# Stage weights of a list-scheduled kernel changed, and one expert matrix's high halves moved from GpSimd to ScalarE

## The chip, the cores and the metric

The kernel runs on one core of a Trainium2 chip. The time is the device time of one execution, in microseconds. The engines are named as in the profile: PE (TensorE, its matmuls), PEld (its weight loads), DVE (VectorE), ACT (ScalarE), POOL (GpSimd) and SP (SyncE, which here only issues transfers). Each runs its own instructions strictly in the order in which they stand in its queue.

## The reference

All inputs are float32. Three stages follow each other.

```python
# 1: delta-rule attention, B=2, H=8, S=768, D=48
k_n = k / (norm(k) + 1e-6)
for t in range(S):
    y[:, :, t] = q_t @ state
    state += beta_t * outer(k_t, v_t - state.T @ k_t)
# 2: gated MLP with mixing over the sequence, d_model 384, d_ff 1024
u, v = split(gelu_tanh(x @ w_in))
x = x + (u * (w_sg @ (layernorm(v) * g_ln) + b_sg)) @ w_out
# 3: one of 8 experts per token, 384 -> 1024 -> 384
e = argmax(x @ w_gate), or the expert of the token before it
    where sigmoid(x @ w_local) >= 0.5
out = p[e] * (relu(x @ w1[e]) @ w2[e])
```

## The kernel before

**One program, ordered by a planner.** The code does not issue instructions as it is written. Each operation is recorded in a `Plan` with its engine, an estimated cost and what it depends on, and at the end `emit()` places all of them, engine by engine. Whenever an engine is free it takes, of the operations that could start within 120 ns of the earliest, the one with the highest sum of its rank (the length of the chain of work that hangs on it) and its bias. The bias is a number per stage, from the table `BIAS`, set by `at(name)` or by the steps of the attention. Every recorded operation carries the line L371 in the profile, so the line tells nothing there, and tiles and shapes have to. All of the working memory is one tile, `arena`, with fixed addresses (`AT`); the matmul banks are `x_80` to `x_85`, a ring of six that all stages share, and two banks `s`.

**Attention.** Time is cut into six tiles of 128 steps. K0 to K5 load and normalise k and make its products, X0 to X2 invert a triangular system on DVE by forward substitution (X0 in blocks of 16, which `join` puts together in T0 and T1), T0 to T5 make the tiles' update matrices on PE, C0 to C5 run the recurrence, and B0 to B2 load beta. W0 to W5 load the six parts of `w_in` and turn them into f16, each with six instructions of 128x512 on DVE through a single raw buffer `w64_512`.

**Halves.** A float32 matmul is made of three f16 matmuls. `split()` makes the two halves: the high half is the value rounded to f16, by the engine that the caller names ("a" is ACT, "p" is POOL, else DVE), and the low half is the rest, for all scaled weights by one `scalar_tensor_tensor` on DVE, which reads the raw tile and the high half.

**MLP and experts.** The stages in0, u0, sp0, out0 do the MLP of the first batch row, in1 to out1 that of the second; prep readies `w_sg` and `w_out`. route0 and route1 build the lists of tokens for each expert; early and late run experts 0 and 1. Then the experts 2 to 6, one more block for an expert with too many tokens (the "list expert", chosen from the data), and expert 7 follow (experts). `load_expert` fetches w1 as three raw tiles of 128x1024 (512 KB) and w2 as four of 128x768 (384 KB), through a ring of three raw buffers, and splits them in pieces of 512 columns: six 128x512 pieces for w1, four 128x512 and four 128x256 for w2. Its operations are the stages load0 (experts 0 and 1) and load (the other seven). Four sets of split weights exist, so an expert's weights can be made while others are used. In `run_blocks`, each of four banks of w1's products takes a relu on ACT, which makes the high half of the hidden values, and a low half on DVE; w2's product is scaled by ACT into `ob`, and POOL writes it to `out` by an indirect DMA (a scatter, `DMA_INDIRECT out_dram<-arena`).

POOL makes the high halves of both matrices, and its queue also holds the gathers and the scatters. The loop over further lists behind the program's main part (`For_i`) runs zero times with this data.

Of the kernel before, what the change touches and what calls it, by code (L numbers as in the profile page):

```python
# [16 lines left out]
def make_split(nc):  # L17
    def split(hi, lo, src, s, he, le):
# [12 lines left out]


ORDER = "K0 K1 B0 X0 K2 K3 B1 X1 T0 T1 C0 C1 K4 K5 B2 X2 T2 T3 C2 C3 T4 T5 C4 C5 W0 W1 W2 W3 W4 W5"
BIAS = {"K0": 5e5, "K1": 5e5, "X0": 4.5e5, "K": 4.5e5, "X": 2e5, "T": 3e5, "C": 4e5, "Q": 3e5, "N": 6e5, "W": 1e5, "B0": 4.7e5, "B": 3e5, "prep": 5e4,
        "in0": 1.4e5, "u0": 1e5, "sp0": 1e5, "out0": 1e5, "in1": 1.2e5, "u1": 8e4, "sp1": 8e4, "out1": 8e4, "load0": -2e5, "route0": 1.5e5, "early": -1e5, "route1": 3e5, "late": -1e5, "list": -2e5,
        "load": -2e5, "gather": 0.0, "experts": 0.0, "rest": -3e5}
SLOTS = 4
WORDS = 46400

# [565 lines left out]
def attention(plan, A, P, q, k, v, beta, x_all, idf, filler):  # L605
# [28 lines left out]

    was, plan.bias = plan.bias, BIAS["N"]
    one = A.tile([128, 1], F32, "one")
# [91 lines left out]
    def stage2(gi):  # L728
# [28 lines left out]
        for j in range(0 if sets[0] in FINE else 31):  # L757
            for eng, lo, hi_, tg, sz in ((nc.vector, 0, min(j + 1, C0), "tmp", TMP), (nc.gpsimd, C0, j + 1, "tmpp", TMPP)):
# [104 lines left out]
    def stage4(b, t):  # L863
# [9 lines left out]
        for c in range(2):  # L873
# [20 lines left out]
            if ci < 2 * NT - 1:  # L894
# [56 lines left out]
def model_kernel(ctx, tc, q, k, v, beta, w_in, g_ln, w_sg, b_sg, w_out, w_gate, w_local, w1, w2, out):  # L951
    nc = tc.nc
    B, H, S, D = q.shape
# [19 lines left out]
    early = ExitStack()  # L973
# [13 lines left out]
    def split(*a):  # L987
        make_split(nc)(*a)
# [306 lines left out]
    def load_expert(fetch, slot, step=512):  # L1295

        W = [ep.tile(SHAPES[nm], F16, tag=f"{nm}{slot}", name=nm, bufs=1) for nm in SHAPES]
        w1h, w1l, w2h, w2l = W
        flat = lambda x: x.rearrange("p a b -> p (a b)")
        for kc in range(KD):  # L1300
            raw = ep.tile([128, F2], F32, tag="raw1", name="raw1", bufs=3)
            fetch(raw, w1, slice(kc * 128, (kc + 1) * 128))
            for c0 in range(0, F2, step):
                cs = slice(c0, c0 + step)
                split(w1h[:, kc, cs], w1l[:, kc, cs], raw[:, cs], 64.0, "p", "v")
        for qd in range(4):
            n = NF2 // 4
            raw = ep.tile([128, F2], F32, tag="raw1", name="raw2", bufs=3)[:, :n * DM].rearrange("p (n d) -> p n d", n=n)
            fetch(raw, w2, slice(qd * n * 128, (qd + 1) * n * 128))
            for c0 in range(0, n * DM, step):  # L1310
                cs = slice(c0, min(c0 + step, n * DM))
                f = lambda x: flat(x[:, qd * n:(qd + 1) * n, :])[:, cs]
                split(f(w2h), f(w2l), flat(raw)[:, cs], 64.0, "p", "v")
        return W
# [4 lines left out]
    def fixed(e):  # L1319
        return lambda raw, w, rs: nc.sync.dma_start(raw, rows_of(w[e], rs))  # L1320
# [57 lines left out]
    def at(name):  # L1378
        plan.bias = BIAS.get(name, 0.0)

# [8 lines left out]
    for b in range(B):  # L1389
# [138 lines left out]
    with tc.For_i(NX, nv, 1) as i:  # L1528
# [5 lines left out]
        X, col = listed(lc, "loop")  # L1534
# [32 lines left out]
```

## Time and profile before

| | |
|---|---|
| time, median of 3 runs | 506.03 us (503.86 to 507.68) |
| the profiled execution | 506.47 us, span 504.8 us |
| busy: PE, DVE, POOL, ACT | 426.8, 363.6, 212.3, 184.1 us |
| mean granted TensorE clock | 0.928 |

The span is the part of an execution that the profiler's instructions cover; 1.7 us lie around it. Attention takes the first 194 us, the MLP runs to about 340 us, routing and the first two experts' blocks overlap it and end at 418 us, and the other experts end at 499 us. A row of a timeline gives the start, the length, the engine, the operation with its operands, and in brackets how long the engine had been idle and what ended that.

### The profile page before, as it was taken

What the parts mean: (1) busy time and instruction counts of PE and PEld (TensorE: products, weight loads), DVE (VectorE), ACT (ScalarE), POOL (GpSimd) and SP (SyncE); (2) the same over time, 40 slices, a digit from 0 to 9 for tenths busy, and PEclk for the clock granted to TensorE, in tenths of its full rate; (3) what the DMA queues carried; (4) which work ended last, traced back from release to release, by engine and by line L of the source; (5) the groups of instructions that cost most, each with busy time, mean ns of one, the idle gap of its engine ahead of it and who ended that gap; (6) DMA issues with size and microseconds to landing.
All of it is one profiled execution on the core that took longest, in us unless ns stands there. A gap on an engine that the chain in (4) does not pass through costs nothing.

```text
span 504.8 us, 16775 instructions
## 1 busy us (share of the span) xinstructions
PE 426.8 (85%) x7100; PEld 325.6 (64%) x7100; DVE 363.6 (72%) x824; ACT 184.1 (36%) x451; POOL 212.3 (42%) x373
## 2 busy tenths in 40 slices
PE   0467689969779899988989799999599999999593
PEld 0466688858769685555645566687488868777372
DVE  1796956689645687989689693678789987647770
ACT  2656335795743644332022241223132213312110
POOL 8413550073000003625476622443557455666551
PEclk9986756899976999989999999999999999999988
DMA  6743201104321543111652400170555466656530
GB/s 95 141 85 67 47 5 21 35 20 126 65 92 44 150 169 116 32 64 32 196 182 105 144 1 32 48 226 32 152 158 165 143 209 173 187 184 204 154 96 26
DMA packets 62191, 53.29 MB, mean 106 GB/s; under 512 B 43549, under 2 KB 55109, under 8 KB 62114
## 3 DMA queue, kind: packets, MB, share of 16 engines
q1 hardware_dynamic: 57730, 46.08, 32.4%
q0 software_dynamic: 2176, 5.71, 3.6%
q8 instruction: 57, 0.93, 0.7%
q10 hardware_dynamic: 2208, 0.40, 0.6%
q14 instruction: 20, 0.16, 0.1%
HBM read 46.27 MB, written 6.89 MB: 105 GB/s over the span
## 4 chain that ended last, share of the span: by engine, by line
PE 55%; DVE 17%; DMA 9%; issue 7%; ACT 4%; POOL 4%; SPq 2%; ACTq 0%; POOLq 0%; DVEq 0%
PE x L371 54%; DVE arena L371 17%; DMA arena<-in_moe_w_dram 4%; ACT arena L371 3%; POOL arena L371 3%; SPq L371 2%; DMA out_dram<-arena 2%; PE s L371 1%; DMA arena<-in_v_dram 1%; DMA arena<-in_moe_w_in_dram 1%; DMA arena<-in_k_dram 1%; DMA arena<-in_moe_w_sg_dram 1%; ACTq L371 0%; DMA arena<-in_beta_dram 0%; DVE x_all L371 0%
## 5 line engine op out<-in xcount | busy, mean ns | idle before, releaser
L371 PE MATMUL x<-arena 64*32 64x32 f32 (+8 forms) x6385 | 372.6, 243 | 45.0 <-DVE arena L371 21.1
L371 PEld LDWEIGHTS <-arena 128*128 128x128 f16 x2005 | 175.7, 99 | 101.0 <-issue 13.6
L371 DVE SCALAR_TENSOR_TENSOR arena<-arena 128x512 f16<-128x512 f32 (+6 forms) x186 | 123.9, 698 | 32.9 <-POOL arena L371 27.2
L371 POOL TENSOR_SCALAR arena<-arena 128x512 f16<-128x512 f32 (+2 forms) x146 | 91.3, 645 | 99.7 <-DVE arena L371 59.5
L371 PEld LDWEIGHTS x<-arena 64*32 64x32 f32 (+3 forms) x4416 | 99.0, 134 | 41.3 <-issue 15.7
L371 ACT ACTIVATE arena<-x 128x384 f16<-128x384 f32 (+5 forms) x137 | 63.5, 483 | 118.0 <-PE x L371 103.5
L371 POOL TENSOR_TENSOR arena<-arena 128x384 f32<-128x384 f32 (+14 forms) x117 | 61.5, 526 | 76.2 <-DVE arena L371 40.1
L371 DVE TENSOR_TENSOR arena<-arena 128x384 f16<-128x384 f32 (+40 forms) x213 | 82.0, 389 | 13.9 <-ACT arena L371 7.4
L371 ACT COPY arena<-x 32x128 f32<-32x128 f32 (+7 forms) x160 | 52.9, 355 | 48.4 <-PE x L371 37.9
L371 DVE SCALAR_TENSOR_TENSOR arena<-x,arena 128x384 f16<-128x384 f32 (+5 forms) x105 | 55.1, 548 | 15.5 <-ACT arena L371 8.1
L371 PE MATMUL x<-idf,arena 128*128 128x128 f32 x183 | 33.8, 332 | 19.6 <-DVE arena L371 19.5
L371 ACT ACTIVATE arena<-arena 128x384 f16<-128x384 f32 (+5 forms) x38 | 19.8, 527 | 59.8 <-POOL arena L371 47.1
L371 PEld LDWEIGHTS x<-idf,arena 128*128 128x128 f32 x183 | 26.4, 172 | 21.5 <-POOL arena L371 17.4
L371 POOL MEMSET arena<- 32x256 f32 (+13 forms) x43 | 14.7, 357 | 58.4 <-DVE arena L371 45.0
L371 DVE TENSOR_SCALAR arena<-arena 128x1 f32<-128x1 f32 (+9 forms) x83 | 25.0, 319 | 15.1 <-DMA arena<-in_beta_dram 8.8
L371 ACT ACTIVATE arena<-x,arena 128x384 f32<-128x384 f32 x17 | 9.8, 580 | 53.2 <-PE x L371 28.1
L371 ACT COPY arena<-arena 64x256 f32<-64x256 f32 (+2 forms) x60 | 26.1, 445 | 5.7 <-DVE arena L371 4.6
L371 POOL DMA_INDIRECT out_dram<-arena x17 | 19.3, 1136 | 19.1 <-ACT arena L371 14.3
L371 DVE TENSOR_TENSOR arena<-arena,x 128x192 f32<-128x192 f32 (+2 forms) x34 | 11.0, 325 | 17.3 <-PE x L371 12.9
L371 POOL DMA_INDIRECT arena<-x2d,arena x15 | 16.9, 1126 | 13.7 <-PE x L371 9.4
L371 DVE STREAM_TRANSPOSE arena<-arena 128x1024 f32<-128x1024 f32 x9 | 17.5, 1978 | 0.2
L371 PE MATMUL s<-arena 64*48 64x48 f32 x352 | 14.1, 223 | 1.2 <-ACT arena L371 1.0
(58 smaller groups left out, 148.6 us busy)
## 6 DMA issues: line engine op xcount, KB each, us to landing
arena<-in_moe_w_dram SPq DMA_DIRECT2D x27, 512.0 KB
arena<-in_moe_w_dram SPq DMA_DIRECT2D x36, 384.0 KB
arena<-in_moe_w_in_dram SPq DMA_DIRECT2D x6, 512.0 KB
arena<-in_v_dram SPq DMA_DIRECT2D x24, 96.0 KB
arena<-in_q_dram SPq DMA_DIRECT2D x24, 96.0 KB
arena<-in_moe_w_sg_dram SPq DMA_DIRECT2D x6, 384.0 KB
x2d<-x_all SPq DMA_DIRECT2D x12, 192.0 KB
arena<-in_k_dram SPq DMA_DIRECT2D x20, 96.0 KB
```

Of the source, the lines that this page charges most:

```text
L371: call(*[real(a) for a in args], **{k: real(a) for k, a in kw.items()})
```

## The change

Some 35 numbers of `BIAS` change, most of them of the attention's steps, which had shared a few numbers before and now have one each. Among the larger moves: K5 rises above K0, K1 falls below K0, B0 falls below the K steps, X2 falls from 2e5 to 27400 (below W0 to W5), in0 and sp0 rise, load rises from -2e5 to -148500, late rises a little and experts falls to -24300. Besides, the high halves of w1 are made on ACT where POOL made them: 54 instructions of 128x512 in the program that runs (nine loads of six).

```diff
-BIAS = {"K0": 5e5, "K1": 5e5, "X0": 4.5e5, "K": 4.5e5, "X": 2e5, "T": 3e5, "C": 4e5, "Q": 3e5, "N": 6e5, "W": 1e5, "B0": 4.7e5, "B": 3e5, "prep": 5e4,
...
-        "load": -2e5, "gather": 0.0, "experts": 0.0, "rest": -3e5}
+BIAS = {"W5": 52900.0, "W4": 104400.0, "W3": 100000.0, "W2": 38000.0, "W1": 100000.0, "W0": 69800.0, "B2": 135000.0, "B1": 395700.0, "C5": 443000.0, "C4": 434500.0, "C3": 408000.0, "C2": 473100.0, "C1": 400000.0, "C0": 397000.0, "T5": 320300.0, "T4": 300000.0, "T3": 300000.0, "T2": 307300.0, "T1": 300000.0, "T0": 300000.0, "X2": 27400.0, "X1": 200000.0, "K5": 646300.0, "K4": 435000.0, "K3": 447700.0, "K2": 450000.0, "K0": 500000.0, "K1": 479300.0, "X0": 4.5e5, "K": 4.5e5, "X": 2e5, "T": 3e5, "C": 4e5, "Q": 300000.0, "N": 600000.0, "W": 1e5, "B0": 417500.0, "B": 3e5, "prep": 50000.0,
...
+        "load": -148500.0, "gather": 0.0, "experts": -24300.0, "rest": -300000.0}
...
-                split(w1h[:, kc, cs], w1l[:, kc, cs], raw[:, cs], 64.0, "p", "v")
+                split(w1h[:, kc, cs], w1l[:, kc, cs], raw[:, cs], 64.0, "a", "v")
```

**At the start**, SP issues before the change four loads of k (K1, K0), four of beta, then the other sixteen of k. After it, all twenty loads of k stand first, the four of K5 in front, and then twelve of beta. ACT, which issues the other halves of K0 and K1, takes K0's first. On DVE, K0's whole normalisation now comes before K1's, and the one operation of X0 that reads beta stands behind K1's reductions instead of ahead of K0's first.

**DVE after X0**, before the change. The first row is the end of X0; the rows from `x_82` to `x_85` with 128x4x64 are the causal masks of C1's products, the transpose of 128x1024 opens X1, and the last row is T0's first step of joining its blocks:

```order
L371 STREAM_TRANSPOSE arena<-arena 128x32x32 x2
L371 TENSOR_TENSOR arena<-arena 128x16 x2
L371 TENSOR_SCALAR arena<-arena 128x16 x2
L371 RECIPROCAL arena<-arena 128x16 x2
L371 TENSOR_TENSOR arena<-x_82,arena 128x4x64
L371 TENSOR_TENSOR arena<-x_83,arena 128x4x64
L371 TENSOR_TENSOR arena<-x_84,arena 128x4x64
L371 TENSOR_TENSOR arena<-x_80,arena 128x4x64
L371 TENSOR_TENSOR arena<-x_81,arena 128x4x64
L371 TENSOR_TENSOR arena<-x_85,arena 128x4x64
L371 STREAM_TRANSPOSE arena<-arena 128x1024
L371 TENSOR_SCALAR arena<-x_82,arena 128x8x16
```

The same place after the change:

```order
L371 STREAM_TRANSPOSE arena<-arena 128x32x32 x2
L371 TENSOR_SCALAR arena<-arena 128x16
L371 RECIPROCAL arena<-arena 128x16 x2
L371 TENSOR_TENSOR arena<-arena 128x16 x2
L371 TENSOR_SCALAR arena<-arena 128x16
L371 RECIPROCAL arena<-arena 128x16
L371 TENSOR_TENSOR arena<-arena 128x16 x2
L371 TENSOR_SCALAR arena<-arena 128x16
L371 RECIPROCAL arena<-arena 128x16
L371 TENSOR_SCALAR arena<-x_82,arena 128x8x16
L371 TENSOR_TENSOR arena<-x_81,arena 128x4x64
L371 TENSOR_TENSOR arena<-x_83,arena 128x4x64
```

T0's step now comes ahead of the masks and of X1. Its next step, the additions, stands behind three operations of X1 instead of 23.

**DVE at the end of X2**, before the change. Rows of 128x2x11 and the like are X2's substitution, `STREAM_TRANSPOSE` of 128x32x32 ends it, rows of 128x192 and 128x4x48 belong to C2 to C4, and rows of 128x512 are the weight steps of W0:

```order
L371 TENSOR_TENSOR arena<-arena,x_82 128x192
L371 TENSOR_TENSOR arena<-arena 128x2x11
L371 TENSOR_TENSOR arena<-arena 128x11 x2
L371 STREAM_TRANSPOSE arena<-arena 128x32x32 x2
L371 TENSOR_TENSOR arena<-arena,x_84 128x192
L371 COPY x_all<-x_85 128x4x48
L371 SCALAR_TENSOR_TENSOR arena<-arena 128x512 x2
L371 TENSOR_SCALAR arena<-arena 128x512
L371 SCALAR_TENSOR_TENSOR arena<-arena 128x512
L371 TENSOR_SCALAR arena<-arena 128x4
L371 TENSOR_TENSOR arena<-arena,x_83 128x192
L371 SCALAR_TENSOR_TENSOR arena<-arena 128x512
```

A place after the change, in the middle of X2, whose substitution goes on behind it for some 50 rows; the rows of 128x512 are those of W1:

```order
L371 TENSOR_TENSOR arena<-arena 128x209
L371 TENSOR_TENSOR arena<-arena 128x19x11
L371 TENSOR_TENSOR arena<-arena 128x198
L371 TENSOR_TENSOR arena<-arena,x_82 128x192
L371 TENSOR_SCALAR arena<-arena 128x512
L371 SCALAR_TENSOR_TENSOR arena<-arena 128x512 x2
L371 TENSOR_TENSOR arena<-arena,x_83 128x192
L371 TENSOR_SCALAR arena<-arena 128x512
L371 TENSOR_TENSOR arena<-x_81,arena 128x4x64
L371 TENSOR_TENSOR arena<-x_80,arena 128x4x64
L371 SCALAR_TENSOR_TENSOR arena<-arena 128x512
L371 TENSOR_TENSOR arena<-arena,x_85 128x192
```

Five of the six 128x512 steps of W0, and all six of W1, move from behind X2 into it. On SP, W1's load moves ahead of C4's loads of q, and W2's ahead of C4's loads of v.

**ACT near the end**, before the change. Rows of 128x512 or 128x2x128 out of a bank are relus, rows of 128x384 with `arena` as second operand are the scaled outputs, and rows of 128x3x128 are gathered tokens:

```order
L371 ACTIVATE arena<-x_83 128x384
L371 ACTIVATE arena<-x_84 128x3x128
L371 ACTIVATE arena<-x_80,arena 128x384
L371 ACTIVATE arena<-x_85,arena 128x384
L371 ACTIVATE arena<-x_81 128x2x128
L371 ACTIVATE arena<-x_83 128x2x128
L371 ACTIVATE arena<-x_84 128x2x128
L371 ACTIVATE arena<-x_80 128x2x128
L371 ACTIVATE arena<-x_85 128x3x128
L371 ACTIVATE arena<-x_82,arena 128x384
L371 ACTIVATE arena<-x_81,arena 128x384
L371 ACTIVATE arena<-x_83 128x512
```

A place near the end after the change, in which the rows of 128x512 out of `arena` are the high halves of w1:

```order
L371 ACTIVATE arena<-arena 128x512 x3
L371 ACTIVATE arena<-x_82,arena 128x384
L371 ACTIVATE arena<-arena 128x512 x2
L371 ACTIVATE arena<-x_80,arena 128x384
L371 ACTIVATE arena<-x_84 128x512
L371 ACTIVATE arena<-x_85 128x512
L371 ACTIVATE arena<-x_83 128x512
L371 ACTIVATE arena<-x_81 128x512
L371 ACTIVATE arena<-x_82 128x2x128
L371 ACTIVATE arena<-x_80 128x2x128
L371 ACTIVATE arena<-arena 128x512 x2
L371 ACTIVATE arena<-x_84,arena 128x384
```

The high halves stand between relus and outputs, in ACT's one queue. On POOL the 54 instructions are gone from between the gathers and the scatters. Relative to PE's work on the experts, the raw loads and their low halves stand two to four raw tiles further ahead than before, and the small operations of the stages list and rest stand later.

## Rows read from the trace of the kernel before

**Rows 1.** The page, first part: busy time of each engine, share of span, instructions.
```profile
PE 426.8 (85%) x7100; PEld 325.6 (64%) x7100; DVE 363.6 (72%) x824; ACT 184.1 (36%) x451; POOL 212.3 (42%) x373
```

**Rows 2.** Busy us of PE, PEld, DVE, ACT, POOL by stretch; clock, DMA share, GB/s.
```profile
132.00:162.00 30.00, 24.05 (x692) 22.02 (x687) 14.15 (x32) 16.80 (x42) 0.00 (x0) 0.77 0.30 82
...
340.00:366.00 26.00, 19.55 (x258) 15.54 (x255) 20.79 (x57) 6.90 (x15) 12.76 (x23) 0.96 0.32 99
366.00:466.00 100.00, 100.00 (x857) 77.19 (x856) 79.07 (x157) 25.73 (x51) 59.99 (x81) 0.99 0.59 176
466.00:497.00 31.00, 24.93 (x194) 17.27 (x191) 18.48 (x27) 6.29 (x14) 16.47 (x23) 0.94 0.38 119
```

**Rows 3.** The chain that ended last, 0 to 34 us: start, length, what.
```profile
3.23 4.80 DMA arena<-in_k_dram
...
8.04 1.89 DMA arena<-in_beta_dram
...
15.15 2.17 DVE arena L371
```

**Rows 4.** Timeline of DVE, 42 to 64 us; idle before each in brackets.
```profile
48.53 2.08 DVE L371 TENSOR_TENSOR arena<-x,arena 128x256 f32<-128x256 f32 x6 [4.14 <-PE x L371]
...
52.41 0.31 DVE L371 TENSOR_SCALAR arena<-x,arena 128x128 f32<-128x128 f32 x1
```

**Rows 5.** Timeline of all engines, 128 to 150 us.
```profile
137.29 0.36 DVE L371 TENSOR_TENSOR arena<-arena,x 128x192 f32<-128x192 f32 x1 [3.26 <-DMA arena<-in_v_dram]
...
142.66 0.43 DVE L371 TENSOR_SCALAR arena<-arena 128x512 int32<-128x512 int32 x1 [0.95 <-DMA arena<-in_moe_w_in_dram]
...
145.93 3.15 PE L371 MATMUL x<-arena 64*64 64x48 f32 x80 [3.54 <-DVE arena L371]
146.45 0.68 DVE L371 SCALAR_TENSOR_TENSOR arena<-arena 128x512 f16<-128x512 f32 x1
```

**Rows 6.** The view of Rows 2, for a stretch of 4 us.
```profile
148.00:152.00 4.00, 4.00 (x105) 4.00 (x104) 0.76 (x2) 1.07 (x3) 0.00 (x0) 0.50 0.12 45
```

**Rows 7.** Groups by line and shape: count, busy us, mean ns, idle before.
```profile
L371 DVE SCALAR_TENSOR_TENSOR arena<-arena 128x512 f16<-128x512 f32 x96 | 77.9, 833 | 29.6 <-POOL arena L371 24.7 <-ACT arena L371 4.5
L371 POOL TENSOR_SCALAR arena<-arena 128x512 f16<-128x512 f32 x102 | 71.2, 709 | 41.9 <-DMA arena<-in_moe_w_dram 36.5 <-DVE arena L371 2.1 <-PE x L371 1.3
...
L371 ACT ACTIVATE arena<-arena 128x512 f16<-128x512 f32 x6 | 3.8, 631 | 2.6 <-DVE arena L371 2.4
```

**Rows 8.** Timeline of all engines, 390.1 to 391.7 us.
```profile
389.28 2.02 POOL L371 TENSOR_SCALAR arena<-arena 128x512 f16<-128x512 f32 x2 [0.94 <-DMA arena<-in_moe_w_dram]
389.72 2.12 DVE L371 SCALAR_TENSOR_TENSOR arena<-arena 128x512 f16<-128x512 f32 x2
```

**Rows 9.** Waits of the whole span: us, times, longest us.
```profile
POOL arena L371 <- DMA arena<-in_moe_w_dram: 36.5, 17, 4.7
```

**Rows 10.** Timeline of all engines, 359 to 366 us.
```profile
361.37 2.22 POOL L371 TENSOR_SCALAR arena<-arena 128x512 f16<-128x512 f32 x3 [3.77 <-DMA arena<-in_moe_w_dram]
...
364.64 1.65 PE L371 MATMUL x<-arena 128*128 128x128 f16 x14 [5.02 <-DVE arena L371]
```

**Rows 11.** Timeline of all engines, 466 to 483 us.
```profile
468.05 3.14 DVE L371 SCALAR_TENSOR_TENSOR arena<-arena 128x512 f16<-128x512 f32 x2 [3.89 <-POOL arena L371]
...
471.45 0.68 DVE L371 SCALAR_TENSOR_TENSOR arena<-arena 128x512 f16<-128x512 f32 x1
...
471.68 4.83 PE L371 MATMUL x<-arena 128*128 128x384 f16 x29 [2.73 <-DVE arena L371]
...
477.24 0.28 PE L371 MATMUL x<-arena 128*128 128x256 f16 x1 [0.73 <-DVE arena L371]
478.42 1.20 POOL L371 TENSOR_SCALAR arena<-arena 128x512 f16<-128x512 f32 x2 [1.78 <-DMA arena<-in_moe_w_dram]
...
479.09 0.39 PE L371 MATMUL x<-arena 128*128 128x256 f16 x2 [1.57 <-POOL arena L371]
...
480.21 3.17 PE L371 MATMUL x<-arena 128*128 128x256 f16 x14 [0.73 <-DVE arena L371]
```

More of the change, by code (lines that the diff above doesn't have):

```diff
@@ L33 @@
 ORDER = "K0 K1 B0 X0 K2 K3 B1 X1 T0 T1 C0 C1 K4 K5 B2 X2 T2 T3 C2 C3 T4 T5 C4 C5 W0 W1 W2 W3 W4 W5"
-BIAS = {"K0": 5e5, "K1": 5e5, "X0": 4.5e5, "K": 4.5e5, "X": 2e5, "T": 3e5, "C": 4e5, "Q": 3e5, "N": 6e5, "W": 1e5, "B0": 4.7e5, "B": 3e5, "prep": 5e4,
-        "in0": 1.4e5, "u0": 1e5, "sp0": 1e5, "out0": 1e5, "in1": 1.2e5, "u1": 8e4, "sp1": 8e4, "out1": 8e4, "load0": -2e5, "route0": 1.5e5, "early": -1e5, "route1": 3e5, "late": -1e5, "list": -2e5,
-        "load": -2e5, "gather": 0.0, "experts": 0.0, "rest": -3e5}
+BIAS = {"W5": 52900.0, "W4": 104400.0, "W3": 100000.0, "W2": 38000.0, "W1": 100000.0, "W0": 69800.0, "B2": 135000.0, "B1": 395700.0, "C5": 443000.0, "C4": 434500.0, "C3": 408000.0, "C2": 473100.0, "C1": 400000.0, "C0": 397000.0, "T5": 320300.0, "T4": 300000.0, "T3": 300000.0, "T2": 307300.0, "T1": 300000.0, "T0": 300000.0, "X2": 27400.0, "X1": 200000.0, "K5": 646300.0, "K4": 435000.0, "K3": 447700.0, "K2": 450000.0, "K0": 500000.0, "K1": 479300.0, "X0": 4.5e5, "K": 4.5e5, "X": 2e5, "T": 3e5, "C": 4e5, "Q": 300000.0, "N": 600000.0, "W": 1e5, "B0": 417500.0, "B": 3e5, "prep": 50000.0,
+        "in0": 359700.0, "u0": 12000.0, "sp0": 173500.0, "out0": 97700.0, "in1": 120000.0, "u1": 89000.0, "sp1": 80000.0, "out1": 47200.0, "load0": -204100.0, "route0": 150000.0, "early": -111300.0, "route1": 300000.0, "late": -68300.0, "list": -2e5,
+        "load": -148500.0, "gather": 0.0, "experts": -24300.0, "rest": -300000.0}
 SLOTS = 4
```

## The prediction

> **What bounds the kernel now.** I read the page first for which engine is full, then busy time by stretch for where it is not, then the chain and timelines for what ends the waits there. PE is busy 426.8 us of the span, DVE 363.6, POOL 212.3, ACT 184.1 [rows 1]. The average hides three kinds of stretch. From 366 to 466 us PE never stops (100.0 of 100), while DVE works 79 us and POOL 60 [rows 2]: nothing that an engine other than PE gains there can be seen in the time, unless it feeds what follows. In attention the limit is a chain of small steps between DVE, PE and ACT: of 132 to 162 us PE is busy only 24 and its clock is granted at 0.77 [rows 2]. And there are two holes behind the MLP, at 340 to 366 us (19.6 of 26 busy) and 466 to 497 us (24.9 of 31) [rows 2], where PE waits for weights. So the change pays, or costs, at the start, at the end of X2, and in the two holes.
>
> The sum is made against the profiled execution, 506.5 us, which stands 0.4 us above the median of 506.0; the difference is left alone. A negative term is a gain.
>
> **The start of attention.** The chain goes from the k load (lands at 8.03) through the beta load (8.04 to 9.93) to DVE, and K0's scaling runs from 15.15 to 17.32 [rows 3]. K0's reduction stands behind an operation that needs beta, and K1's steps are mixed into K0's. With beta's operation and K1 behind it, the chain ahead of the scaling loses the wait behind the k load (some 1 us that ACT's square doesn't already fill) and about 2 us of K1's steps: −3 us. Against that, K5's four loads now stand ahead of K0's on SP's queue. Eight loads of K1 and K0 were the first to move before, and K5's make twelve: of the 4.80 us that a load of K0 took to land [rows 3], 4.80 × 4/12 = 1.6 us is what they can add, an estimate. The twelve beta loads follow sixteen more of k; they are needed when X0 opens, which leaves them 10 us.
>
> Then DVE stands idle for 4.14 us at C1's masks, which wait for PE, works on six of them (2.08 us) and X1's transpose, and does T0's join step at 52.41 [rows 4]. The join needs only X0. In the new order it is first, and four masks follow. If DVE is filled, X1 starts up to 4.1 us sooner; but the masks' inputs come from PE, and part of the wait will merely move behind the join. I count a quarter of it, 1 us. Together −4, bounds −9 (3 + 4.1 + 2 for masks that fall into idle time) and +2 (K5's loads delay K0 by 1.6 and no gain comes).
>
> **W0 and W1 inside X2.** After X2, DVE waits 3.26 us for v and later stands in W1's steps, whose raw weights landed at 142.6; PE waits 3.54 us behind that and goes on at 145.93 [rows 5], at half clock, 0.50 in 148 to 152 us [rows 6]. A mean of 0.77 over 30 us [rows 2] is 0.23 × 30 / 0.5 = 13.8 us at half speed, which cost 6.9 us of PE's time. Moving the weights' steps removes both waits (6.8 us), since the loads of W1 and W2 are issued sooner too. It costs DVE in X2 what the steps take: W1's six run from 142.66 to 147.13 with others between them, 3.6 us of their own [rows 5] (the first and the last of the six); with five of W0, 6.6 us. X2 is DVE's own chain, so I let all of them count and the waits cancel them, and take 2 of the 6.9 us of half clock back: −2. Bounds: −13.7 (X2's idle gaps swallow the added steps, waits and half clock all go) and +7 (the steps count and the waits stay, for another reason).
>
> **High halves from POOL to ACT.** A low half on DVE takes 0.68 us in a stretch without a POOL piece beside it [rows 11] (at 471.45) and 1.06 where POOL's pieces run throughout, which then take 1.01 [rows 8]. Over all 96 the mean is 0.833 [rows 7], so 96 × 0.153 = 14.7 us of DVE time come from this, and 54 of 90 pieces belong to w1: some 8.8 us. ACT's own price is 54 × 0.631 = 34 us [rows 7], on an engine with 320 us idle. Most of both falls where PE is full, so it buys nothing directly: −1. Bounds: −4 (half of the 8.8 shows where PE waits for weights) and +4 (relus ahead of w2's products wait behind two pieces, 1.26 us, three times).
>
> The Trainium skill ("SBUF — State Buffer", section "Who interferes with whom") says that a DVE instruction with two SBUF inputs contends with a GpSimd one that reads SBUF, that the shared port is an exclusive lock, and that ACT never waits for it. The trace agrees on the contention, not on a full block: a blocked low half would take its 0.68 and POOL's piece, about 1.39 by the mean of POOL's pieces, against 1.06 measured. By the lock alone the freed DVE time would be up to twice as large, and this term at its lower bound, −4.
>
> **The hole at 359 to 365 us.** PE waits 5.02 us; POOL got its raw tile of w1 at 361.37 after 3.77 us of waiting for the DMA, and DVE stood behind POOL with the gathered tokens' low half behind it [rows 10]. The same low half stays behind weight pieces on DVE, 24 of them against 20 before, since the loads run further ahead. 0, bounds −5 (the raw is there in time) and +3 (four more pieces of 0.68).
>
> **The tail.** POOL's pieces stand behind a scatter that waits for ACT, so DVE gets its first low half at 468.05 after 3.89 us idle and PE stops for 2.73; then w1 of the last expert comes so late that PE stops for 0.73, 1.57 and 0.73 us more while POOL waits for the DMA [rows 11]. That is 5.8 us. Now w1 doesn't pass POOL's queue, and the raw tiles are asked for two to four tiles sooner: at 512 KB and the 176 GB/s of the stretch before [rows 2], one tile is 3 us, so two are more than these stops. w2 still passes POOL. −5, bounds −6 and 0.
>
> **Sum.** −4 − 2 − 1 + 0 − 5 = −12; 506.5 − 12 = **494.5 us**. The far ends don't come together: as the root of their squares the distances to the lower ones (5, 11.7, 3, 5, 1) make 14 us, to the upper ones (6, 9, 5, 3, 5) 13. These are ends; three quarters of them give the forecast's own range, 484 to 505.
>
> **The rivals.** A change within 1% (5 us) is about what a measurement of this kernel can't tell from none: 501 to 511 counts as the same.
> *Same.* What attention gains is given back, because in0 and sp0 must wait for the weights and for prep, which are now ordered differently, and PE runs nearly full from 195 us on. The tail is then the one term left, −5, and the relus take back part of it: 501 to 508, taken as 504. For it: 100.0 of 100 us in the longest stretch [rows 2]. Against it: PE-bound work doesn't absorb an earlier start; it moves with it.
> *Faster still.* PE is fed evenly through the end of attention and the half clock of 132 to 162 us goes whole: another 4.9 us, and DVE's 4.14 us at the masks goes too, another 3: about 486, or 482 with the hole at 359 us closed. For it: the clock fell right after PE had stood idle, 3.54 us and then 0.50 [rows 5, 6]. Against: the first half of attention stays a chain.
> *Slower.* ACT's in-order queue now waits for w1 from memory, with relus behind. POOL waited 36.5 us in 17 waits for raw tiles, 4.7 at the longest [rows 9]; three of an expert's seven tiles are w1, so 36.5 × 3/7 = 15.6 us of waits move to ACT. A hidden layer's last relu is what w2's first product needs, so a wait there stops PE unless another block's products stand between. If all of it reaches PE, and the tail gains nothing: 506.5 − 7 + 15.6 = 515. It decides from the point where a w1 tile lands later than the relu behind it becomes ready. Against it: the tiles are asked for sooner, and the order puts a piece where its tile is expected, with six banks of slack on PE. The stops before W2 need only be a third of 15.6 to end at no gain.
>
> **How the numbers follow.** Forecast 0.48 (485 to 501 in the main), faster still 0.14, same 0.22, slower 0.16. That makes faster by over 1% 0.62, within 1% 0.22, slower by over 1% 0.16 (each case with its centre's side). For eight times in ten the range leaves out the lower half of the faster case and the upper half of the slower one: 481 to 512.
>
> **What the profile after would show.** The start is right if K0's scaling ends about 3 us before 17.3 and X1's transpose starts by 47; X2 is right if PE has no stop of 3 us between the end of X2 and the end of attention and the latter comes 5 us or more before 194. ACT's pieces are harmless if waits of ACT for the expert weights sum to a few microseconds and PE stays full from 366 to 466. The tail is right if the four stops behind 466 us shrink to 1 us together. Wrong would be: attention ending where it did, since its waits have other causes than the order; a low granted clock in a new place; or long waits of ACT for w1 with PE idle beside them.

## The result, and the profile after

The changed kernel takes 485.39 us (median of 4 runs, 483.87 to 488.42) against 506.33 us of the kernel before beside it: a ratio of 0.9599, 95% interval 0.9535 to 0.9663. All ratios here leave out executions that took over 1.5% longer than the fastest of the same kernel. The profiled execution has a span of 486.7 us, 18.1 less than before. The first part of its page, to be held against [rows 1]:

```profile
PE 427.5 (88%) x7100; PEld 329.3 (68%) x7100; DVE 349.3 (72%) x824; ACT 211.8 (44%) x505; POOL 177.7 (37%) x319
```

PE's work is the same; DVE has 14 us less, POOL 35 less, ACT 28 more. A span is PE's busy time and its idle time, so the 18.1 us are 18.8 us less of idle (59.2 against 78.0) and 0.6 more of busy. Where the idle time went is read from busy time by stretch. First the kernel before, in stretches that both share (busy us of PE, PEld, DVE, ACT and POOL; then clock, DMA share, GB/s):

```profile
0.00:60.00 60.00, 31.22 (x1238) 27.99 (x1239) 39.49 (x108) 30.64 (x86) 27.12 (x73) 0.86 0.50 91
60.00:132.00 72.00, 61.15 (x2260) 55.57 (x2261) 55.48 (x156) 43.25 (x130) 24.26 (x72) 0.81 0.15 37
132.00:200.00 68.00, 58.76 (x1461) 49.82 (x1455) 42.60 (x97) 35.22 (x85) 3.14 (x6) 0.90 0.39 116
200.00:300.00 100.00, 91.52 (x563) 55.00 (x561) 84.52 (x170) 25.62 (x51) 53.40 (x75) 0.98 0.29 96
300.00:370.00 70.00, 63.26 (x609) 46.73 (x607) 46.84 (x118) 18.15 (x40) 30.60 (x51) 0.98 0.32 101
370.00:460.00 90.00, 90.00 (x743) 68.98 (x741) 72.89 (x149) 23.73 (x47) 53.45 (x71) 1.00 0.59 172
460.00:504.80 44.80, 30.93 (x248) 21.48 (x245) 21.82 (x32) 7.54 (x15) 20.34 (x29) 0.91 0.36 113
```

The same view of the changed kernel:

```profile
0.00:60.00 60.00, 29.89 (x1272) 26.92 (x1272) 39.07 (x104) 27.73 (x82) 28.12 (x75) 0.78 0.49 85
60.00:132.00 72.00, 63.51 (x2144) 57.81 (x2141) 53.76 (x141) 46.01 (x135) 24.18 (x64) 0.75 0.24 60
132.00:200.00 68.00, 63.81 (x1559) 53.91 (x1559) 48.83 (x120) 38.36 (x91) 5.27 (x11) 0.90 0.30 86
200.00:300.00 100.00, 100.00 (x643) 61.25 (x642) 84.30 (x187) 36.31 (x71) 44.25 (x63) 1.00 0.34 106
300.00:370.00 70.00, 62.03 (x622) 48.09 (x621) 45.97 (x109) 21.34 (x47) 29.60 (x45) 0.93 0.46 140
370.00:460.00 90.00, 90.00 (x737) 68.23 (x735) 68.92 (x150) 37.96 (x73) 40.91 (x56) 1.00 0.62 184
460.00:486.70 26.70, 18.21 (x136) 13.06 (x134) 8.41 (x16) 4.13 (x7) 5.33 (x7) 0.89 0.14 45
```

The length of a stretch less PE's busy time is PE's idle time:

| stretch, us | before | after | gain |
|---|---|---|---|
| 0 to 60 | 28.8 | 30.1 | -1.3 |
| 60 to 132 | 10.9 | 8.5 | 2.4 |
| 132 to 200 | 9.2 | 4.2 | 5.0 |
| 200 to 300 | 8.5 | 0.0 | 8.5 |
| 300 to 370 | 6.7 | 8.0 | -1.3 |
| 370 to 460 | 0.0 | 0.0 | 0.0 |
| from 460 | 13.9 | 8.5 | 5.4 |

So the first 60 us give nothing, 60 to 200 gives 7.4, the MLP 8.5 and the tail 5.4. The clock did not help: its mean is 0.906 against 0.928, and 0.78 and 0.75 in the first two stretches against 0.86 and 0.81.

One execution doesn't settle a stretch to the microsecond. Two of the experiments below (high halves on ACT alone, and with the experts' numbers) have the same order on DVE, ACT and POOL as the kernel before up to 198 us. PE's idle time from 60 to 200 us is 15.9 and 20.6 us in them, against 20.1 before, with a granted clock from 60 to 132 us of 0.72 and 0.83, against 0.81. A second execution of the changed kernel has 10.4 where this one has 12.7.

The start, in the timeline of DVE of the changed kernel (start, length, engine, operation; idle time before it in brackets):

```profile
13.38 0.96 DVE L371 TENSOR_TENSOR arena<-arena 128x768 f32<-128x768 f32 x1
...
21.27 0.98 DVE L371 TENSOR_SCALAR arena<-arena 128x32 f32<-128x32 f32 x1 [0.67 <-DMA arena<-in_beta_dram]
```

```profile
46.39 0.26 DVE L371 TENSOR_SCALAR arena<-x,arena 128x128 f32<-128x128 f32 x1
...
47.89 1.97 DVE L371 STREAM_TRANSPOSE arena<-arena 128x1024 f32<-128x1024 f32 x1
...
61.26 0.35 DVE L371 TENSOR_SCALAR arena<-x,arena 128x128 f32<-128x128 f32 x1 [4.75 <-PE x L371]
```

K0's scaling ends at 14.34 where it ended at 17.32 [rows 3], and the wait for beta is 0.67 us at 21.27. But X0 needs the products of K1 as well as those of K0, and K1's scaling, on POOL, starts at 17.01 instead of 15.03 (both rows are shown further below). X0's first transpose starts at 26.28 instead of 27.72; then DVE waits 1.51 us for ACT, before a step of a later tile's normalisation that now stands inside X0, and X0's last two transposes start no sooner. Before the change and after it:

```profile
39.10 3.86 DVE L371 STREAM_TRANSPOSE arena<-arena 128x1024 f32<-128x1024 f32 x2
```

```profile
31.76 0.17 DVE L371 TENSOR_SCALAR arena<-arena 128x16 f32<-128x16 f32 x1 [1.51 <-ACT arena L371]
...
39.24 3.93 DVE L371 STREAM_TRANSPOSE arena<-arena 128x1024 f32<-128x1024 f32 x2
```

T0's join step comes at 46.39 instead of 52.41 [rows 4] and X1's transpose at 47.89, 2.7 us before the 50.6 at which the masks of [rows 4] end. Since X0 ends where it did, this comes from the order of the join and the masks. But at 61.26 DVE waits 4.75 us for PE, before the third of the four joins (T0's and T1's, one for each batch row), with X1 behind it. X1's last two transposes start at 96.02, where they started at 96.07: the gain is used up. (In the second execution of the changed kernel they start at 91.31.)

The start and the end of X2 in the timeline of DVE, before the change and after it:

```profile
92.14 1.96 DVE L371 STREAM_TRANSPOSE arena<-arena 128x1024 f32<-128x1024 f32 x1
...
127.22 3.90 DVE L371 STREAM_TRANSPOSE arena<-arena 128x1024 f32<-128x1024 f32 x2
```

```profile
101.02 1.94 DVE L371 STREAM_TRANSPOSE arena<-arena 128x1024 f32<-128x1024 f32 x1
...
144.17 3.87 DVE L371 STREAM_TRANSPOSE arena<-arena 128x1024 f32<-128x1024 f32 x2
```

X2 ends 17 us later. Of these, 9 are its later start, behind X1's end instead of ahead of it; from its first transpose to the end of its last it takes 47.0 us, where it took 39.0. The waits of [rows 5], 3.26 us of DVE for v and 3.54 of PE, are not in the changed trace, and PE's longest stop between the end of X2 and the end of attention is 0.73 us. Attention itself does not end sooner. Its last copy into `x_all`, before and after:

```profile
194.28 0.35 DVE L371 COPY x_all<-x 128x192 f32<-128x192 f32 x1
```

```profile
198.92 0.35 DVE L371 COPY x_all<-x 128x192 f32<-128x192 f32 x1
```

In the second execution of the changed kernel it stands at 190.95. The first product of in0 starts at 172.3 us instead of 184.8, so that PE has work of the MLP between attention's.

PE's timeline from 440 us on, where [rows 11] shows four stops:

```profile
439.78 18.20 PE L371 MATMUL x<-arena 128*128 128x256 f16 x177
457.83 0.83 PE L371 MATMUL x<-idf,arena 128*128 128x128 f32 x6
458.49 19.72 PE L371 MATMUL x<-arena 128*128 128x384 f16 x144
```

It runs without a stop to 478.2; the 8.5 us behind 460 are what follows the last matmul. The hole of [rows 10] is there in another form:

```profile
316.35 0.55 PE L371 MATMUL x<-idf,arena 128*128 128x128 f32 x3 [1.93 <-DMA arena<-x2e,arena]
...
346.61 0.55 PE L371 MATMUL x<-idf,arena 128*128 128x128 f32 x3 [0.67 <-DMA arena<-x2d,arena]
349.58 0.55 PE L371 MATMUL x<-idf,arena 128*128 128x128 f32 x3 [2.42 <-DMA arena<-x2d,arena]
...
353.31 5.41 PE L371 MATMUL x<-arena 128*128 128x128 f16 x53 [2.53 <-DVE arena L371]
```

Two stops of 0.67 and 2.42 us wait for gathers, and one of 2.53 us for DVE, with another of 1.93 us at 316. And the waits of ACT and POOL for expert weights, of all waits of the span (us, times, longest us):

```profile
POOL arena L371 <- DMA arena<-in_moe_w_dram: 21.0, 11, 4.5
...
ACT arena L371 <- DMA arena<-in_moe_w_dram: 4.3, 4, 1.6
```

POOL's 36.5 us [rows 9] are 21.0, and ACT waits 4.3 us in all, 1.6 at the longest.

### The profile page after: what moved, and what is told of

The parts are those of the page before. It is cut to its first block, busy times and chain, and to the rows that moved or that the text cites. A ratio compares the mean times of both kernels' runs of the same rounds, so it can differ in the third digit from the quotient of the medians.

```text
span 486.7 us, 16780 instructions
## 1 busy us (share of the span) xinstructions
PE 427.5 (88%) x7100; PEld 329.3 (68%) x7100; DVE 349.3 (72%) x824; ACT 211.8 (44%) x505; POOL 177.7 (37%) x319
## 5 line engine op out<-in xcount | busy, mean ns | idle before, releaser
L371 PE MATMUL x<-arena 64*32 64x32 f32 (+9 forms) x6385 | 374.7, 248 | 23.8 <-issue 12.6
L371 PEld LDWEIGHTS <-arena 128*128 128x128 f16 (+1 forms) x2005 | 176.1, 99 | 85.6 <-issue 5.0
L371 DVE SCALAR_TENSOR_TENSOR arena<-arena 128x512 f16<-128x512 f32 (+7 forms) x186 | 115.0, 649 | 29.7 <-POOL arena L371 15.1
L371 PEld LDWEIGHTS x<-arena 64*32 64x32 f32 (+3 forms) x4416 | 102.9, 140 | 30.6 <-issue 16.1
L371 ACT ACTIVATE arena<-x 128x384 f16<-128x384 f32 (+5 forms) x137 | 62.9, 482 | 84.6 <-PE x L371 80.1
L371 POOL TENSOR_TENSOR arena<-arena 128x384 f32<-128x384 f32 (+14 forms) x117 | 64.4, 550 | 64.6 <-DVE arena L371 44.0
L371 DVE TENSOR_TENSOR arena<-arena 128x16 f32<-128x16 f32 (+42 forms) x213 | 78.8, 372 | 10.8 <-ACT arena L371 4.7
L371 POOL TENSOR_SCALAR arena<-arena 128x512 f16<-128x512 f32 (+3 forms) x92 | 54.3, 606 | 76.3 <-DVE arena L371 51.4
L371 ACT ACTIVATE arena<-arena 128x512 f16<-128x512 f32 (+4 forms) x92 | 51.3, 583 | 59.5 <-POOL arena L371 43.5
L371 ACT COPY arena<-x 32x128 f32<-32x128 f32 (+7 forms) x160 | 52.0, 354 | 45.3 <-PE x L371 41.3
L371 DVE SCALAR_TENSOR_TENSOR arena<-x,arena 128x384 f16<-128x384 f32 (+6 forms) x105 | 55.3, 548 | 18.6 <-ACT arena L371 17.4
L371 PE MATMUL x<-idf,arena 128*128 128x128 f32 x183 | 33.0, 329 | 25.7 <-DVE arena L371 16.5
L371 PEld LDWEIGHTS x<-idf,arena 128*128 128x128 f32 x183 | 25.6, 170 | 28.6 <-POOL arena L371 18.4
L371 POOL DMA_INDIRECT out_dram<-arena x17 | 18.6, 1094 | 41.9 <-ACT arena L371 32.8
L371 POOL MEMSET arena<- 32x256 f32 (+13 forms) x43 | 14.7, 356 | 48.7 <-DVE arena L371 47.4
L371 ACT ACTIVATE arena<-x,arena 128x384 f32<-128x384 f32 x17 | 9.9, 580 | 50.3 <-PE x L371 43.7
L371 DVE TENSOR_SCALAR arena<-arena 128x1 f32<-128x1 f32 (+9 forms) x83 | 26.3, 325 | 7.4 <-POOL arena L371 2.7
L371 ACT COPY arena<-arena 64x256 f32<-64x256 f32 (+2 forms) x60 | 26.4, 445 | 1.2
L371 DVE TENSOR_TENSOR arena<-arena,x 128x192 f32<-128x192 f32 (+2 forms) x34 | 11.0, 325 | 20.7 <-PE x L371 20.0
L371 POOL DMA_INDIRECT arena<-x2d,arena x15 | 15.7, 1047 | 26.2 <-PE x L371 22.9
L371 DVE TENSOR_REDUCE arena<-arena 128x16 f32<-128x768 f32 (+4 forms) x17 | 9.4, 551 | 12.5 <-ACT arena L371 12.1
L371 DVE STREAM_TRANSPOSE arena<-arena 128x1024 f32<-128x1024 f32 x9 | 17.6, 1992 | 0.2
```

What stands on the lines that cost most here:

```text
L371: call(*[real(a) for a in args], **{k: real(a) for k, a in kw.items()})
```

## The experiments

Theory A, formed from the tables above: the new order makes the gain, by feeding PE with MLP work at the end of attention and in the MLP, and by loading the experts' weights sooner. Theory B: POOL's pieces beside DVE's low halves were the cost, and moving them to ACT makes the gain. All ratios below are to the kernel before on the same chip, with 95% intervals. Of the table, 30 numbers differ in effect; the diffs show only the entries that differ in a run, and the rest of the table stays as before.

**ACT alone.**

```diff
-                split(w1h[:, kc, cs], w1l[:, kc, cs], raw[:, cs], 64.0, "p", "v")
+                split(w1h[:, kc, cs], w1l[:, kc, cs], raw[:, cs], 64.0, "a", "v")
```

> The table of before, only the high halves of w1 on ACT. Theory A (the order makes the gain: MLP work fills PE's holes at the end of attention and between 200 and 300 us, and earlier loads close the tail): only the stop of 2.7 us at 469 us and part of the other stops of the tail can go, 502 to 506 us. Theory B (POOL's pieces beside DVE's low halves were the cost, and taking them off the shared path makes the gain): most of the 21 us, 493 us or less.

Measured: 0.994 (0.988 to 1.000). Theory B falls: what ACT alone gives is between nothing and 30% of the whole (0 to 1.2 of 4.0%). Its trace shows why it is no loss either, and what it lacks. From its waits, its groups by shape, and the timeline of PE (the experiments' table stands on fewer lines, so L371 is L369 there):

```profile
ACT arena L369 <- DMA arena<-in_moe_w_dram: 31.9, 11, 7.3
```

```profile
L369 DVE SCALAR_TENSOR_TENSOR arena<-arena 128x512 f16<-128x512 f32 x96 | 70.0, 751 | 30.3 <-ACT arena L369 19.9 <-POOL arena L369 10.3
```

```profile
471.60 4.66 PE L369 MATMUL x<-arena 128*128 128x384 f16 x29 [0.32 <-DVE arena L369]
476.60 0.28 PE L369 MATMUL x<-arena 128*128 128x256 f16 x1 [0.33 <-DVE arena L369]
478.63 0.39 PE L369 MATMUL x<-arena 128*128 128x256 f16 x2 [1.75 <-ACT arena L369]
479.36 14.96 PE L369 MATMUL x<-arena 128*128 128x256 f16 x112 [0.34 <-DVE arena L369]
```

The low halves fall from 833 ns [rows 7] to 751, 7.9 us of DVE; but ACT now waits 31.9 us for w1, 7.3 at the longest. That is the mechanism of the slower rival, and with the old order it is there. PE has cover for it up to the tail (from 370 to 460 us its idle time is 0.0), where four stops of 2.7 us together remain of 5.8.

**The table alone.**

```diff
-BIAS = {"K0": 5e5, "K1": 5e5, ...
+BIAS = {"W5": 52900.0, "W4": 104400.0, ...
```

> The new table, the high halves of w1 still on POOL. Theory A: nearly all of the gain stays, 485 to 491 us, PE without a stop from 200 to 300 us, and some of the tail's stops back. Theory B: the gain is lost, 500 us or more, with low halves of 0.83 us mean again.

Measured: 0.971 (0.964 to 0.977). In the main as theory A has it: 2.9 of the 4.0% stay, although the low halves take 0.857 us on average. Two parts of it did not come true: from 200 to 300 us PE's idle time is 2.5 us, not nothing, and the tail's stops are not back. PE has no stop behind 440 us here either, with the high halves on POOL, so the table closes the tail; which of its numbers do is seen below. What ACT adds to the table is the difference to 0.960, about 1%, where the intervals touch. Against the last run below, the changed kernel at 0.957 (0.951 to 0.962) on the chip of this run, it is 1.4%, and they do not touch.

**Attention's numbers alone, and the rest with ACT.**

```diff
+"W0": 69800.0, "W2": 38000.0, "W4": 104400.0, "W5": 52900.0, "X2": 27400.0,
+"K1": 479300.0, "K3": 447700.0, "K4": 435000.0, "K5": 646300.0, "B0": 417500.0,
+"B1": 395700.0, "B2": 135000.0, "T2": 307300.0, "T5": 320300.0,
+"C0": 397000.0, "C2": 473100.0, "C3": 408000.0, "C4": 434500.0, "C5": 443000.0
```

> Only the numbers of the attention's steps (K, X, T, C, B, W) are new, the later stages' are old, high halves on POOL. Theory A: attention's own end does not come sooner (194 to 197 us) and in0 starts no sooner than before, so 501 to 508 us. The prediction on record had put 6 us of gain into these numbers: 498 to 501 us. Theory B: 506 us.

Measured: 0.978 (0.969 to 0.987). Here theory A was wrong as I had put it: attention's numbers carry about half of the gain by themselves, and attention's last copy starts at 185.8 us, 8.5 sooner. Busy time by stretch:

```profile
60.00:132.00 72.00, 65.05 (x2166) 59.73 (x2160) 53.92 (x143) 46.39 (x135) 24.47 (x65) 0.73 0.25 61
132.00:200.00 68.00, 65.22 (x1521) 54.48 (x1517) 50.00 (x117) 35.02 (x83) 10.97 (x18) 0.87 0.31 91
200.00:300.00 100.00, 92.68 (x582) 56.26 (x580) 82.17 (x182) 27.32 (x56) 49.48 (x72) 0.97 0.31 99
```

PE's idle time is 7.0 us from 60 to 132 and 2.8 from 132 to 200, against 10.9 and 9.2; from 200 to 300 it stays at 7.3.

```diff
-"in0": 1.4e5, "u0": 1e5, "sp0": 1e5, "out0": 1e5, "u1": 8e4, "out1": 8e4,
+"in0": 359700.0, "u0": 12000.0, "sp0": 173500.0, "out0": 97700.0, "u1": 89000.0, "out1": 47200.0,
-"load0": -2e5, "early": -1e5, "late": -1e5, "load": -2e5, "experts": 0.0
+"load0": -204100.0, "early": -111300.0, "late": -68300.0, "load": -148500.0, "experts": -24300.0
-                split(w1h[:, kc, cs], w1l[:, kc, cs], raw[:, cs], 64.0, "p", "v")
+                split(w1h[:, kc, cs], w1l[:, kc, cs], raw[:, cs], 64.0, "a", "v")
```

> Only the numbers of the stages behind attention are new, and the high halves of w1 are on ACT; attention's numbers are old. Theory A: PE's holes between 200 and 300 us (8.5 us) and the tail's stops (4.6 us) go, 489 to 495 us. If attention's numbers carried the gain: 500 us or more. Theory B: as e1.

Measured: 0.980 (0.968 to 0.992), with runs from 485 to 498 us. The other half, then: the two ratios multiply to 0.959, the whole, though each is known only to about 1% either way. Idle from 200 to 300 us is 2.2 us, as theory A had it, and the tail's 8.4.

**The start alone.**

```diff
-"K0": 5e5, "K1": 5e5, "K": 4.5e5, "B0": 4.7e5,
+"K0": 5e5, "K1": 479300.0, "K3": 447700.0, "K4": 435000.0, "K5": 646300.0, "B0": 417500.0,
```

> Only K1, K3, K4, K5 and B0 are new (the order of the loads and of K0 against K1); high halves on POOL. The prediction on record counted 4 us for the start, 3 of them for K0 ahead of K1: ratio 0.992. The theory after the result: K1's products, not K0's, open X0, so X0 ends where it did (43 us) and the ratio is 1.00; no better than 0.997.

Measured: 0.995 (0.990 to 0.999). Between the two expectations. Its first 60 us have 31.1 us of idle (28.8 before), so the half per cent is not made at the start; it stands in no stretch clearly. X0's last two transposes start at 40.02 us, no sooner than before, as the theory after the result has it.

**X2 and W alone.**

```diff
-"X": 2e5, "W": 1e5,
+"X2": 27400.0, "W0": 69800.0, "W2": 38000.0, "W4": 104400.0, "W5": 52900.0
```

> Only X2 and W0, W2, W4, W5 are new (the steps on the weights of w_in inside X2); high halves on POOL. If these carry what attention's numbers gained: idle time of PE from 60 to 200 us falls from 20 to some 13 us or less, ratio 0.980 to 0.990. The prediction on record had -2 us, 0.996. If the smaller numbers of C, T and B carry it: 1.00.

Measured: 0.987 (0.982 to 0.992). Busy time by stretch:

```profile
60.00:132.00 72.00, 63.47 (x2254) 58.55 (x2254) 55.80 (x152) 43.50 (x128) 25.31 (x68) 0.74 0.19 46
132.00:200.00 68.00, 64.18 (x1515) 50.86 (x1512) 51.89 (x122) 38.27 (x90) 12.89 (x23) 0.97 0.34 102
```

Idle from 60 to 200 is 12.3 us, against 15.9 to 20.6 in the executions with the old order, and 12.7 is what the changed kernel has. Attention's last copy starts at 185.7 us, 8.6 sooner. By the ratio, these five numbers carry more than half of attention's gain (1.3 of 2.2%).

**The MLP's numbers, and the experts', each with ACT.**

```diff
+"in0": 359700.0, "u0": 12000.0, "sp0": 173500.0, "out0": 97700.0, "u1": 89000.0, "out1": 47200.0
-                split(w1h[:, kc, cs], w1l[:, kc, cs], raw[:, cs], 64.0, "p", "v")
+                split(w1h[:, kc, cs], w1l[:, kc, cs], raw[:, cs], 64.0, "a", "v")
```

> Only in0, u0, sp0, out0, u1 and out1 are new, and the high halves are on ACT. If the MLP's numbers close the holes of 200 to 300 us: idle there falls from 5.9 us (high halves on ACT with the table of before) to 2 us or less, ratio 0.982 to 0.988, against 0.994 for ACT alone. If they don't: 0.994.

Measured: 0.973 (0.968 to 0.978), more than was expected; idle from 200 to 300 is 3.0 us, not quite the 2 expected, and from 460 on 8.4. PE has no stop behind 440 us, although the numbers of load and experts are the old ones.

```diff
+"load0": -204100.0, "early": -111300.0, "late": -68300.0, "load": -148500.0, "experts": -24300.0
-                split(w1h[:, kc, cs], w1l[:, kc, cs], raw[:, cs], 64.0, "p", "v")
+                split(w1h[:, kc, cs], w1l[:, kc, cs], raw[:, cs], 64.0, "a", "v")
```

> Only load0, early, late, load and experts are new, and the high halves are on ACT. The tail's stops go (13.9 us of idle behind 460 us to some 8.5; 11.6 with ACT alone), the rest stays: ratio 0.985 to 0.990. If the tail needs the earlier stages' new order: 0.994, as with ACT alone.

Measured: 0.984 (0.978 to 0.989). The ratio is what was expected of a closed tail, but the tail is not closed: idle from 460 on is 10.7 us (11.6 with ACT alone), with stops of 1.19, 0.33 and 0.39 us. The first of them:

```profile
467.52 0.39 PE L369 MATMUL x<-arena 128*128 128x256 f16 x2 [1.19 <-ACT arena L369]
```

The rest of the ratio stands in no stretch clearly. So beside the high halves on ACT it is the MLP's numbers that close the tail, and not those of load and experts. What goes with them is how early the last expert's loads are issued. The first one stands 35.2 us ahead of the end of PE's last matmul with the MLP's numbers, 35.6 in the changed kernel and 33.6 with the table alone, where PE doesn't stop; it stands 32.5 us ahead before the change, 29.1 with ACT alone and 27.6 with the experts' numbers, where PE stops.

**One number.**

```diff
-"u0": 1e5,
+"u0": 12000.0,
-                split(w1h[:, kc, cs], w1l[:, kc, cs], raw[:, cs], 64.0, "p", "v")
+                split(w1h[:, kc, cs], w1l[:, kc, cs], raw[:, cs], 64.0, "a", "v")
```

> One number of the table: u0 from 100000 to 12000, and the high halves on ACT. In the order of its build the transposes of w_sg then stand ahead of u0's and in1's products, as in the changed kernel. If the late transposes are what makes sp0 wait, the idle time of PE from 200 to 300 us falls from 5.9 us (ACT alone) to 3 us or less, and the ratio is 0.985 to 0.990. If the holes have another cause (in0's late start): idle as with ACT alone, ratio 0.994.

Measured: 0.982 (0.978 to 0.987). Busy time from 200 to 300 us in ACT alone and in this run, which differ by this number:

```profile
200.00:300.00 100.00, 94.12 (x560) 56.27 (x559) 80.69 (x172) 35.53 (x70) 40.13 (x57) 0.97 0.32 107
```

```profile
200.00:300.00 100.00, 99.44 (x637) 60.82 (x636) 83.20 (x174) 34.11 (x67) 42.69 (x60) 1.00 0.30 95
```

Idle falls from 5.9 to 0.6 us, so this number closes the MLP's holes. With u0 below prep (50000), the transposes of `w_sg` stand ahead of the last of u0's and of in1's products in the order: the last of them runs at 192 us instead of 235. That their low halves on DVE were what sp0 waited for is read from that and from the waits of PE for DVE, and was not tried by itself. It can't be all of it, for the longest of the stops with ACT alone waits for the logits, behind the MLP's output; it is 0.44 us with u0's number. Two of these stops, in ACT alone:

```profile
222.37 1.01 PE L369 MATMUL x<-idf,arena 128*128 128x128 f32 x6 [1.26 <-DVE arena L369]
...
283.45 0.91 PE L369 MATMUL x<-idf,x_all 128*128 128x128 f32 x3 [2.60 <-DVE logit L369]
```

Idle from 132 to 200 us falls too, from 8.3 to 4.5, with the old numbers of X2 and W: the end of attention can be filled in more than one way, so the gains of the parts need not add up. The tail is not this number's: PE still stops for 0.72, 0.30 and 1.75 us, from 449 to 457 us, since this execution ends sooner.

**Combinations.**

```diff
+"X2": 27400.0, "W0": 69800.0, "W2": 38000.0, "W4": 104400.0, "W5": 52900.0,
+"in0": 359700.0, "u0": 12000.0, "sp0": 173500.0, "out0": 97700.0, "u1": 89000.0, "out1": 47200.0
-                split(w1h[:, kc, cs], w1l[:, kc, cs], raw[:, cs], 64.0, "p", "v")
+                split(w1h[:, kc, cs], w1l[:, kc, cs], raw[:, cs], 64.0, "a", "v")
```

> The two sets that gained most by themselves: the numbers of X2 and W and those of the MLP, with the high halves on ACT; start, C, T, B and the experts' numbers are old. If the parts add up (1.3% and 2.7%): 0.960, the whole of the change. If both fill the same holes around 200 us: 0.968 to 0.973.

Measured: 0.975 (0.970 to 0.979), short of both expectations and no better than the MLP's numbers alone (0.973, on another chip). Busy time from 132 to 200 us:

```profile
132.00:200.00 68.00, 59.19 (x1366) 45.28 (x1362) 54.39 (x131) 39.11 (x92) 10.32 (x20) 0.97 0.30 90
```

The idle time from 132 to 200 is back, 8.8 us, as in the run with the MLP's numbers (9.0).

```diff
+"load0": -204100.0, "early": -111300.0, "late": -68300.0, "load": -148500.0, "experts": -24300.0
```

> As the run before, with the numbers of load0, early, late, load and experts too. Added up: 0.950, better than the changed kernel. If the tail is closed by ACT and the MLP's order already (8.4 us of idle behind 460 us in that run): the same as the run before.

Measured: 0.970 (0.966 to 0.974): hardly more than the run before, to which the lines above were added, and not the 0.950 of the sum.

The last run is the changed kernel itself, with the whole of the diff.

> The changed kernel once more, beside the others on the same chip: 0.960 as measured before, within its interval of 0.953 to 0.966.

Measured: 0.957 (0.951 to 0.962), beside the two on the same chip. So the numbers of the start, C, T and B, which the run before lacks, are worth 1.3% in the presence of the others. Idle from 132 to 200 is 3.5 us here against 8.8 there. Attention's last copy starts at 191.0 us here, and at 209.6 in the run before, 207.6 in the one before that, and 214.2 with the MLP's numbers alone: without the numbers of the start, C, T and B, the raised in0 pushes attention's end back. Which of them hold it was not tried; since in0 rises by far, to 359700, it is likely the numbers of C4 and C5, which rise with it and keep the recurrence ahead, but that is argued and not shown. No version tried beats the changed kernel.

## Why the prediction was right, and where it was not

The forecast of 494.5 us had the sign right and the time 9 us too high: 12 us of gain forecast, 21 measured by the medians, within the range and at the lower end of the forecast's own. Its parts fared worse than its sum; that the errors of the first two cancel is luck. By its steps:

- **The start, -4: wrong.** PE's idle time there rose by 1.3 us, and the start's numbers alone leave it at 31.1. The step that failed is the 3 us: K0's scaling did end 3.0 us sooner, but I let all that follows move with it, and X0 needs K1 too, whose scaling came 2.0 us later. X0's last transposes start at 39.24 instead of 39.10. The 1 us counted behind X0 was there at first (X1 starts 2.7 us sooner, at 47.89, where the sign asked for 47), and then DVE's wait at the masks only moved to the third join, where it is 4.75 us: PE's products for that join came no sooner than 61 us.
- **W0 and W1 inside X2, -2: mis-sized, and by another path.** It measured 7.4 us of PE's idle time from 60 to 200 us, 7.8 with X2's and W's numbers alone. The waits went as said, and X2 itself became 8 us longer, near the 6.6 counted. But I had counted X2's end as attention's end, and let the added steps cancel the waits. With X2's and W's numbers alone attention ends 8.6 us sooner, although X2 ends 9.6 us later. In the changed kernel attention ends 4.6 us later in the one execution and 3.3 sooner in the other, where the sign asked for 5 us sooner, and the time falls all the same, since PE has in0's products from 172.3 us on. The half clock that I gave back moved on: the mean from 132 to 162 us is 0.86 instead of 0.77, from 162 to 195 us it is 0.92 instead of 1.00, and from 132 to 200 us 0.90 in both.
- **High halves on ACT, -1: right with the old order, too small with the new one.** ACT alone gave 0.6% or 3 us (interval 0 to 6), and DVE's low halves gave 7.9 us of the 8.8 forecast. Beside the new table it gave 1 to 1.4%, 5 to 7 us, past the bound of -4, with 7.3 us of low halves (80.4 us with the table alone, 73.1 in the changed kernel). PE's idle time does not show where: it is 60.1 us with the table alone, and 59.2 and 57.7 in the two executions of the changed kernel.
- **The hole at 359 us, 0: about right**, 1.3 us worse.
- **The tail, -5: right**, 5.4 us, and by the cause that was named second: the raw tiles are asked for sooner. The table alone closes it, with the high halves still behind POOL's scatters. It is the MLP's numbers that bring the loads forward, though, and not load's own.
- **What the sum left out: the MLP, 8.5 us.** This is nearly all of the 9 us missed, since the errors of the start and of X2 cancel. I wrote that PE runs nearly full from 195 us on and priced nothing there; the stretch from 200 to 300 us had 8.5 us of idle, and one number, u0's, takes 5.3 of the 5.9 that ACT leaves.

Of the rivals, "faster still" named the time (486) for a reason that did not occur, which is luck: the half clock moved on and did not go (the mean of the whole fell), and so did DVE's wait. "Same" fell with the MLP. "Slower" is real as a mechanism: with the old order ACT waits 31.9 us for w1. It waits 16.5 with the experts' numbers, 13.7 with the MLP's, 5.9 with the MLP's, X2's and W's, and 4.3 with the whole table, and PE's cover in the expert phase hides it in either order.

Of the signs of being wrong, two appeared in the first execution: attention ended no sooner, and the clock was lower in a new place, the first 132 us (0.78 and 0.75; 0.83 in both stretches in the second execution). The time fell beside them because the MLP's work moved, which no sign watched.

The Trainium skill ("SBUF — State Buffer", section "Who interferes with whom") has a DVE instruction with two SBUF inputs contend with a GpSimd one that reads SBUF, and calls the shared port pair an exclusive lock. K0's scaling, a product of two SBUF tiles, took 2.17 us before [rows 3], with POOL's scaling of K1 beside it from 15.03, and takes 0.96 us at 13.38 in the changed kernel, with that one at 17.01:

```profile
15.03 1.47 POOL L371 TENSOR_TENSOR arena<-arena 128x768 f32<-128x768 f32 x1 [2.98 <-ACT arena L371]
```

```profile
17.01 1.48 POOL L371 TENSOR_TENSOR arena<-arena 128x768 f32<-128x768 f32 x1 [3.35 <-ACT arena L371]
```

POOL's product takes as long in both. Held up until POOL's ends at 16.50, K0's would end at 17.46; it ended at 17.32. Here the trace is close to the section's exclusive lock, and 1.2 of the 3.0 us by which K0's scaling ends sooner would be this, which the sum did not count. For the low halves the trace is not of one kind: beside the 1.06 us of [rows 8], which the prediction took, the first of the two at 468.05 in [rows 11] took 2.40 us, with six of POOL's pieces running from 467.39 on:

```profile
468.05 2.40 DVE L371 SCALAR_TENSOR_TENSOR arena<-arena 128x512 f16<-128x512 f32 x1 [3.89 <-POOL arena L371]
```

## What to carry to other kernels

Set PE's idle time out by stretch for the whole program before pricing a change of order, and give every stretch that has any a term; a stretch at 92% is worth as much as a visible hole. A longer chain on one engine costs only as much as the engine that sets the end then lacks work, so ask what runs beside it before counting its length. Moving work to an engine with idle time is safe only if what it waits for arrives early: here ACT waited 31.9 us with one order and 4.3 with another. Where one step's end opens the next stage, ask what else that stage needs: K0 came 3 us sooner and X0 did not.

## What was not expected of the hardware

The same 7100 matmuls take a different busy time from one execution to the next, with the granted clock. The changed kernel took 427.5 us at a mean clock of 0.906 in the execution shown above and 420.8 at 0.927 in the second; ACT alone took 435.3 at 0.899. From their pages, the changed kernel's second execution and ACT alone:

```profile
PE 420.8 (88%) x7100; PEld 322.7 (67%) x7100; DVE 349.7 (73%) x824; ACT 212.2 (44%) x505; POOL 178.5 (37%) x319
```

```profile
PE 435.3 (87%) x7100; PEld 335.1 (67%) x7100; DVE 347.2 (69%) x824; ACT 212.5 (42%) x505; POOL 172.0 (34%) x319
```

The execution of ACT alone that was profiled took 504.9 us, with a median of 498.05. The profiled execution with u0's number took 484.7 us, less than the 488.4 of the changed kernel's first, while its median is 491.6, against 485.4 and 480.1 for the changed kernel. A profile's span by itself can thus mislead by as much as a good part of this change is worth. PE's idle time is not free of the clock either: with one order up to 198 us, it was 15.9 us from 60 to 200 us where the clock from 60 to 132 us was 0.72, and 20.6 where it was 0.83. So the idle time says where to look, and the medians decide.
